# Attention and four experts on one core: where the weights' maxima come from, when preparations and chunk scales are issued, and a head's scores in one run

## The chip, the cores and the metric

The kernel runs on one core of one Trainium2 chip. The metric is the device time of one execution in microseconds (us); lower is better. The engines are named as in the profile: PE is TensorE (PEld is its weight load), DVE is VectorE, ACT is ScalarE, POOL is GpSimd, SP is SyncE, which here issues the DMAs.

## The reference

```python
def _attn_ref(q, k, v, f):                  # B, H, S, D = 4, 8, 576, 64
    scores = scale * np.matmul(q, k.transpose(0, 1, 3, 2))
    cum = np.cumsum(np.log(np.clip(f, 0.0001, 1.0)), axis=-1)
    decay = cum[:, :, :, None] - cum[:, :, None, :]
    scores = np.where(causal, -1000000000.0, scores + decay)
    attn = np.exp(scores - np.max(scores, axis=-1, keepdims=True))
    attn = attn / (np.sum(attn, axis=-1, keepdims=True) + 1e-09)
    return np.matmul(attn, v)

def _moe_ref(x, domain_probs, w1, w2):      # N, D, E, F = 2304, 512, 4, 1024
    p = domain_probs / (domain_probs.sum(-1, keepdims=True) + 1e-09)
    for e in range(E):
        h = np.maximum(x @ w1[e], 0.0)
        out += p[:, e:e + 1] * (h @ w2[e])
```

The attention output, heads side by side, is the x of the second function. The experts are dense: every row goes through all four.

## The kernel before

**Precision.** Each fp32 product is made of three passes: every operand is split into a high part and a low remainder, and high*high, high*low and low*high are added in PSUM. In the first sweep the parts are in the 32-bit matmul format; later they are 16-bit halves, which need scales that are powers of two. A scale comes from a maximum over the tensor: one per expert's weights (w_peek loads parts of the weights a second time, w_scale works the maxima out), one per chunk of x (x_scale).

**Attention.** A job is a batch, a pair of heads and one half of the queries: the first 256 rows (half 0, score tiles t = 0, 1) or the last 320 (half 1, t = 2, 3, 4 with 384, 512 and 576 keys). For a head, `prep` (L563 to L578) makes the high and low parts of q and k: hi on ACT, q2 (`q`, one buffer for each of the two heads of a pair), kl and the low part on POOL. `qk_pe` (L618) makes a tile's scores, two matmuls for each piece of columns, in a PSUM bank of the pool ps_a, which has four and also serves transposes, attention products and chunk scales. `qk_min` (L632) takes scores plus mask to SBUF and finds the minimum on DVE, `qk_exp` (L647) the exponential on ACT, `turn16` (L716, L717) scaled 16-bit copies, and SP issues DMA transposes of them (L726). `av_pair` (L818) multiplies with v two heads later.

**Experts.** x is cut into nine chunks of 256 rows. A step is a chunk, a pair of hidden units' blocks and its two matmul layers: `l1` (L1013), `gate` (relu and split on ACT and DVE, L1026 and L1027) and `l2` (L1046); DVE adds the scaled result to the chunk's accumulator (L1073). The first sweep (28 steps) runs chunks 0 to 2 in the 32-bit format with the attention of half 0; the second (52 steps) runs chunks 1 to 4 in halves with the attention of half 1. Then chunks 5 to 8 go through a stage of their own (L1284), which the change does not touch. `w_split` (L953 to L981) prepares a weight unit from its raw load `wr`, three buffers; units 0 to 31 are the first sweep's.

**Order.** The attention's pieces stand in a list (asteps), each with a cost; `pace` emits as many of them between two expert matmul groups as the costs and the chunks' due places allow. A tile framework then schedules each engine's instructions, and `tc.issue_after(i)` keeps what is issued inside behind instruction i on i's engine. `behind` and `paced` use it with a step's gate; `lows` are POOL's last preparations. When a chunk is complete, its `turn` enters the list:

```python
            (50, lambda: (top(), across())),
            (50, exponent),
            (150, finish),
```

Here top is the chunk's maximum on DVE (L261), across its transpose on PE into a row (L200, tile topx), exponent the power of two on DVE and a matmul that spreads it (L221). The steps at which expert e's weights are read for their maxima start at `PEEK = (1, 15, 31, 45)`, 16 steps each; 17 steps after each start w_scale reduces, stores and reads back the maxima (dw, tops).

## Time and profile before

| what | value |
|---|---|
| median of 3 runs | 925.6 us (924.88 to 925.85) |
| profiled execution, its own time | 930.58 us |
| span of its trace, first to last instruction | 928.8 us |
| mean granted clock of TensorE | 0.991 |
| instructions | 16629 |
| DMA | 159.45 MB, 172 GB/s in the mean |

The profiled execution is one run with the profiler on; its trace is what the rows below come from. A busy share is a mean over stages with different limits, so the windows and waits say more than the table of engines. An instruction's duration on PE includes its way through the array, so matmuls overlap: what one costs is read from start to start. In brackets behind an instruction stands the idle time of its engine before it, and what ended it.

### The profile page before, as it was taken

Reading aid. Unit: us, or ns where it says so; the run is one execution under the profiler, and the core shown is the slowest. Engines: PE = TensorE matmul, PEld = TensorE weight load, DVE = VectorE, ACT = ScalarE, POOL = GpSimd, SP = SyncE. Lnnn points to the kernel's source line nnn. Section 1 sums busy time; section 2 is a strip of 40 time slices with the busy share of each in tenths; the row PEclk is TensorE's granted clock in tenths of the full one; section 3 lists DMA queues with packets and bytes.
Section 4 is the critical chain, followed back from the end, with each engine's and each line's share of the span. In section 5 each row is a group of like instructions: output and inputs, shape, how many; then the busy total and the mean of one; then the engine's idle time right before and its main releaser. Section 6 shows DMA issues by size and latency. Waiting matters only on the chain.

```text
span 928.8 us, 16629 instructions
## 1 busy us (share of the span) xinstructions
PE 882.4 (95%) x5783; PEld 620.7 (67%) x5783; DVE 710.0 (76%) x1458; ACT 569.3 (61%) x1137; POOL 528.0 (57%) x528
## 2 busy tenths in 40 slices
PE   4899989998998899999999999899998999999998
PEld 3699879898876567666666666554455654666547
DVE  5768766686998888799888887676678647786487
ACT  5868766557676567767767775555665345653350
POOL 4655675655555552455635673785778527885060
PEclk9999989999999999999999999999999999999999
DMA  7457755455979969889999996744323324232003
GB/s 266 144 165 260 260 176 151 159 166 166 262 186 220 283 166 246 219 168 255 265 261 214 262 229 167 246 172 148 115 69 103 125 68 136 68 116 67 23 1 92
DMA packets 147508, 159.45 MB, mean 172 GB/s; under 512 B 86148, under 2 KB 107328, under 8 KB 147424
## 3 DMA queue, kind: packets, MB, share of 16 engines
q1 hardware_dynamic: 147424, 158.39, 61.1%
q8 instruction: 45, 0.74, 0.3%
q14 instruction: 39, 0.32, 0.1%
HBM read 117.30 MB, written 21.65 MB: 150 GB/s over the span
## 4 chain that ended last, share of the span: by engine, by line
PE 55%; POOL 12%; DVE 10%; ACT 7%; DMA 7%; issue 4%; SPq 0%; ACTq 0%; POOLq 0%; DVEq 0%
PE l L1046 16%; PE l L1013 15%; PE y L1284 8%; PE m L1284 7%; PE s L618 4%; POOL s L1344 4%; POOL wt L1178 3%; PE o L818 2%; POOL wu L1178 1%; DMA wr<-in_w 1%; DMA pk<-in_w 1%; DVE acc L1073 1%; DVE z L717 1%; DMA vr<-in_v 1%; ACT wt L1205 1%
## 5 line engine op out<-in xcount | busy, mean ns | idle before, releaser
L1013 PE MATMUL l<-y,w 128*128 128x256 f16 x1248 | 154.8, 275 | 2.7 <-ACT w L980 1.9
L647 ACT ACTIVATE p<-p,nm 128x576 f32<-128x576 f32 (+3 forms) x160 | 95.7, 599 | 82.7 <-DVE nm L632 77.9
L1013 PEld LDWEIGHTS <-w 128*128 128x128 f16 x1248 | 118.4, 99 | 34.2 <-issue 7.1
L1046 PE MATMUL l<-w,gh 128*128 128x512 f16 x408 | 122.2, 382 | 2.7 <-DVE acc L1073 2.0
L564 POOL CAST q<-raw 64x320 fp32r<-64x320 f32 (+1 forms) x56 | 28.1, 502 | 149.6 <-PE s L618 148.2
L1073 DVE SCALAR_TENSOR_TENSOR acc<-y,scg,acc 128x256 f32<-128x256 f32 (+1 forms) x164 | 81.1, 515 | 14.9 <-PE y L1284 14.7
L717 DVE SCALAR_TENSOR_TENSOR z<-p,rs,z 128x384 f16<-128x384 f32 (+3 forms) x128 | 82.4, 665 | 12.7 <-ACT z L716 11.3
L1284 PE MATMUL m<-rh,bs 128*128 128x512 f16 x256 | 86.6, 379 | 0.0
L572 POOL TENSOR_TENSOR kl<-raw,hi 64x576 fp32r<-64x576 f32 (+1 forms) x56 | 66.5, 1188 | 33.8 <-ACT hi L563 28.3
L618 PE MATMUL s<-hi 128*128 128x384 f32 (+1 forms) x192 | 74.9, 394 | 11.3 <-DVE hi L578 8.9
L632 DVE CUSTOM_DVE_ANT_0 p<-s,mask 128x288 f32<-128x288 f32 (+2 forms) x160 | 74.4, 473 | 13.3 <-PE s L618 12.7
L1210 POOL TENSOR_TENSOR bs<-wt,bs 128x512 f16<-128x512 f32 x32 | 38.1, 1192 | 71.3 <-ACT bs L1209 71.1
L1046 PE MATMUL l<-w,gl 128*128 128x512 f16 x204 | 77.3, 382 | 0.0
L716 ACT ACTIVATE z<-p,rs 128x384 f16<-128x384 f32 (+3 forms) x128 | 69.4, 589 | 7.0 <-DVE rs L678 3.4
L1027 DVE SCALAR_TENSOR_TENSOR gl<-l,gh 128x512 f16<-128x512 f32 (+1 forms) x80 | 54.8, 685 | 16.5 <-ACT gh L1026 15.8
L1013 PE MATMUL l<-xh,wh 128*128 128x256 f32 x224 | 65.1, 293 | 0.9 <-ACT xh L859 0.9
L957 POOL TENSOR_TENSOR wl<-wr,wh 128x512 fp32r<-128x512 f32 x48 | 61.7, 1313 | 7.3 <-ACT wh L953 3.6
L1284 PE MATMUL m<-rh,bw 128*128 128x512 f16 x191 | 64.4, 379 | 1.4 <-ACT r L1330 1.4
L1013 PE MATMUL l<-xl,wh 128*128 128x256 f32 x224 | 65.3, 292 | 0.0
L618 PE MATMUL s<-kl,q 66*128 66x384 f32 (+1 forms) x192 | 63.2, 334 | 2.2 <-DMA kl<-nc 2.2
L1013 PE MATMUL l<-xh,wl 128*128 128x256 f32 x224 | 65.2, 292 | 0.1
L1284 PEld LDWEIGHTS <-bs 128*128 128x128 f16 x384 | 37.6, 98 | 38.4
(385 smaller groups left out, 2344.0 us busy)
## 6 DMA issues: line engine op xcount, KB each, us to landing
wr<-in_w SPq DMA_DIRECT2D x90, 512.0 KB
pk<-in_w SPq DMA_DIRECT2D x64, 256.0 KB
wd<-w SPq DMA_DIRECT2D x32, 512.0 KB
raw<-in_qk SPq DMA_DIRECT2D x32, 448.0 KB
bw<-wd SPq DMA_DIRECT2D x32, 256.0 KB
bv<-wd SPq DMA_DIRECT2D x32, 256.0 KB
raw<-in_qk SPq DMA_DIRECT2D x24, 256.0 KB
vp<-in_v SPq DMA_DIRECT2D x10, 512.0 KB
```

Source lines behind the costliest of these rows:

```text
L572: eng.tensor_tensor(out=kl[:64, :wk], in0=r[:64, ko : ko + wk], in1=hi[:64, ko : ko + wk].bitcast(F32), op=ALU.subtract,)
L618: nc.tensor.matmul(out=ps[:, at : at + z - a], lhsT=lhsT, rhs=rhs, start=(m == 0), stop=(m == 1),)
L632: nc.vector.tensor_tensor_reduce(out=pt[:, a:z], in0=ps, in1=mask[:, m0 + a : m0 + z], scale=-0.125, scalar=BIG if n == 0 else nm[:, col : ...
L647: nc.scalar.activation(out=pt[:, :w_], in_=pt[:, :w_], func=AF.Exp, scale=-1.0, bias=self.nmax[hh][:, c : c + 1], accum_out=self.ssum[:, h ...
L716: nc.scalar.activation(out=o[:, 0], in_=x, func=AF.Copy, scale=sc)
L717: nc.vector.scalar_tensor_tensor(out=o[:, 1], in0=x, scalar=sc, in1=o[:, 0], op0=ALU.mult, op1=ALU.subtract)
L957: eng.tensor_tensor(out=wl[n][:, a:z], in0=r[:, a:z], in1=wh[n][:, a:z].bitcast(F32), op=ALU.subtract,)
L1013: nc.tensor.matmul(out=self.l1p[:, fi, :], lhsT=lhsT, rhs=rhs[:, k, :], start=(k == 0 and m == 0), stop=(k == 3 and m == 2),)
L1027: self.last = nc.vector.scalar_tensor_tensor(out=self.gl, in0=self.l1p, scalar=0.0, in1=self.gh.bitcast(F32) if wide else self.gh, op0=ALU ...
L1046: matmul(out=l2[tt], lhsT=lhsT, rhs=rhs, start=(self.ps == 0 and fi == 0 and m == 0), stop=(self.ps == 1 and fi == 1 and m == 2),)
L1073: nc.vector.scalar_tensor_tensor(out=acc[c][:, tt, d0:d1], in0=ps, scalar=sc, in1=acc[c][:, tt, d0:d1], op0=ALU.mult, op1=ALU.add,)
L1284: line.append(nc.tensor.matmul(**args))
```

## The change

Four things are edited. The weights of experts 2 and 3 are no longer loaded a second time for their maxima: w_split reduces the raw unit while it is in SBUF for the first sweep, and w_scale follows at steps 37 and 42. `prep` and `prep_v` are put behind the gate of the step before and behind POOL's last preparation. The chunk scale's chain has costs between its parts, and its PE instructions go behind the last l1 matmul so far. For half 1 a head's scores of all three tiles are issued in one run (`qk_head`), with the fourth bank saved: tile 4 is cut at key 448, and its last 128 columns share tile 2's bank.

```diff
--- before.py
+++ after.py
@@ -28,7 +28,8 @@
     ((1, 2, 3, 4), (1, 2, 3, 4), (2, 3, 4), (3, 4)),
 )
 WIDE = (0, 1, 2)
-PEEK = (1, 15, 31, 45)
+PEEK = (1, 15)
+SCALE = (18, 32, 37, 42)
 V_PEEK = 1
 PT = ("ptx", "pth", "ptl")
 TURN = ((1, 14), (2, 18), (3, 24), (4, 28))
@@ -482,12 +483,17 @@
                 out=yl[c], in0=xl[c].bitcast(F32), scalar=sc, in1=yl[c], op0=ALU.mult, op1=ALU.add
             )
 
+    def spaced(f):
+        with tc.issue_after(experts[-1].ins):
+            f()
+
     def turn(c):
 
         top, across, exponent, finish = x_scale(c, (c,))
         return [
-            (50, lambda: (top(), across())),
-            (50, exponent),
+            (0, top),
+            (900, lambda: spaced(across)),
+            (600, lambda: spaced(exponent)),
             (150, finish),
         ]
 
@@ -597,33 +603,38 @@
                 self.ssum = st_p.tile([128, 2, n], F32, tag="ssum", name=f"ss{self.nm}")
                 self.rs = st_p.tile([128, 2, n], F32, tag="rs", name=f"rs{self.nm}")
 
+        def qk_bank(self, hh, t):
+            return ps_a.tile([128, 512], F32, tag="a", name=f"s{self.nm}_{hh}_{t}")
+
+        def qk_piece(self, hh, t, a, z, ps):
+
+            o, i = self.qo + TOK0[t] - self.q0, TOK0[t] - self.q0
+            for m, (lhsT, rhs) in enumerate(
+                (
+                    (self.hi[hh][:, o : o + 128], self.hi[hh][:, self.ko + a : self.ko + z]),
+                    (q2[hh][:, i : i + 128], self.kl[hh][:66, a:z]),
+                )
+            ):
+                nc.tensor.matmul(out=ps, lhsT=lhsT, rhs=rhs, start=(m == 0), stop=(m == 1))
+            self.sp.setdefault((hh, t), []).append((a, z, ps))
+
         def qk_pe(self, hh, its):
 
             at = 512
             for t in its:
-                o = self.qo + TOK0[t] - self.q0
                 w_ = TOK0[t] + 128
-                cuts = ((0, w_),) if w_ <= 512 else ((0, w_ // 2), (w_ // 2, w_))
-                for n, (a, z) in enumerate(cuts):
-                    if at + z - a > 512:
-                        ps = ps_a.tile([128, 512], F32, tag="a", name=f"s{self.nm}_{hh}_{t}_{n}")
-                        at = 0
-                    i = TOK0[t] - self.q0
-                    for m, (lhsT, rhs) in enumerate(
-                        (
-                            (self.hi[hh][:, o : o + 128], self.hi[hh][:, self.ko + a : self.ko + z]),
-                            (q2[hh][:, i : i + 128], self.kl[hh][:66, a:z]),
-                        )
-                    ):
-                        nc.tensor.matmul(
-                            out=ps[:, at : at + z - a],
-                            lhsT=lhsT,
-                            rhs=rhs,
-                            start=(m == 0),
-                            stop=(m == 1),
-                        )
-                    self.sp.setdefault((hh, t), []).append((a, z, ps[:, at : at + z - a]))
-                    at += z - a
+                if at + w_ > 512:
+                    ps, at = self.qk_bank(hh, t), 0
+                self.qk_piece(hh, t, 0, w_, ps[:, at : at + w_])
+                at += w_
+
+        def qk_head(self, hh):
+
+            two, three, four = (self.qk_bank(hh, t) for t in (2, 3, 4))
+            self.qk_piece(hh, 2, 0, 384, two[:, :384])
+            self.qk_piece(hh, 4, 448, 576, two[:, 384:])
+            self.qk_piece(hh, 3, 0, 512, three)
+            self.qk_piece(hh, 4, 0, 448, four[:, :448])
 
         def qk_min(self, hh, t):
             pt, nm, col = self.p[hh, t], self.nmax[hh], 2 * (t - self.its[0])
@@ -889,10 +900,10 @@
 
         st = []
         if FIRST < n < len(heads) and heads[n][1] == 0:
-            st.append((0, heads[n][0].prep_v))
+            st.append((0, lambda j=heads[n][0]: held(j.prep_v)))
         if n + 1 < len(heads):
             j, hh = heads[n + 1]
-            st.append((0, lambda j=j, hh=hh: j.prep(hh)))
+            st.append((0, lambda j=j, hh=hh: held(lambda: j.prep(hh))))
         if n + 2 < len(heads):
             j, hh = heads[n + 2]
             st.append((0, lambda j=j, hh=hh: j.far(hh)))
@@ -900,8 +911,13 @@
         qs, ts, us = [], [], []
         if n < len(heads):
             j, hh = heads[n]
+            if j.half:
+                qs.append((1400, lambda j=j, hh=hh: j.qk_head(hh)))
             for t in j.its:
-                qs.append((TOK0[t] + 328, lambda j=j, hh=hh, t=t: j.qk_tile(hh, t)))
+                if j.half:
+                    qs.append((224, lambda j=j, hh=hh, t=t: (j.qk_min(hh, t), j.qk_exp(hh, t))))
+                else:
+                    qs.append((TOK0[t] + 328, lambda j=j, hh=hh, t=t: j.qk_tile(hh, t)))
             if j.half:
                 qs.append((0, lambda j=j, hh=hh: j.recip16(hh)))
                 for t in j.its:
@@ -910,7 +926,7 @@
                 qs.append((0, j.recip))
         if n - 2 >= FIRST and heads[n - 2][1] == 1 and heads[n - 2][0].half:
             j = heads[n - 2][0]
-            qs[2:2] = [(1000, j.av_pair), (0, j.out16)] + ready(n - 2)
+            qs[3:3] = [(1000, j.av_pair), (0, j.out16)] + ready(n - 2)
         if n - 2 >= FIRST and heads[n - 2][0].half == 0:
             j, hh = heads[n - 2]
             late_ = [(200, lambda j=j, hh=hh: j.av(hh))]
@@ -951,6 +967,14 @@
             wh[n] = w_p.tile([128, 1024], F32R, tag="wh", name=f"wh{n}")
             wl[n] = w_p.tile([128, 1024], F32R, tag="wl", name=f"wl{n}")
             nc.scalar.activation(out=wh[n], in_=r, func=AF.Copy)
+            if n // 8 >= len(PEEK):
+                nc.vector.tensor_reduce(
+                    out=wmax[:, :, n % 8, n // 8],
+                    in_=r.rearrange("p (k c) -> p k c", k=2),
+                    op=ALU.max,
+                    axis=AX.X,
+                    apply_absolute_value=True,
+                )
             eng = nc.vector if n in W_DVE else nc.gpsimd
             for a in (0, 512):
                 z = a + 512
@@ -993,6 +1017,7 @@
 
     acc = {}
     l2 = {}
+    experts = []
 
     class Step:
         def __init__(self, s, g, c, ps):
@@ -1010,13 +1035,14 @@
                 a = wh[n][:, k * 128 : (k + 1) * 128]
                 z = wl[n][:, k * 128 : (k + 1) * 128]
                 for m, (lhsT, rhs) in enumerate(((a, th), (a, tl), (z, th))):
-                    nc.tensor.matmul(
+                    i = nc.tensor.matmul(
                         out=self.l1p[:, fi, :],
                         lhsT=lhsT,
                         rhs=rhs[:, k, :],
                         start=(k == 0 and m == 0),
                         stop=(k == 3 and m == 2),
                     )
+            experts.append(i)
 
         def gate(self):
             wide = self.s == 0
@@ -1618,6 +1644,12 @@
     for n in range(len(W_SLOT), 6):
         w_split(n)
 
+    def held(f):
+        if prev is None:
+            f()
+        else:
+            paced(prev, f)
+
     def paced(t, f):
         with tc.issue_after(t.first.ins), tc.issue_after(t.last.ins), tc.issue_after(lows[-1].ins):
             f()
@@ -1631,10 +1663,10 @@
         for e, first_ in enumerate(PEEK):
             if 0 <= n - first_ < 16:
                 w_peek(e, n - first_)
-            if n == first_ + 17:
-                a_, b_ = w_scale(e)
-                behind(a_)
-                at_step(n + 3, b_)
+        if n in SCALE:
+            a_, b_ = w_scale(SCALE.index(n))
+            behind(a_)
+            at_step(n + 3, b_)
         if 0 <= n - V_PEEK < NV:
             v_peek(n - V_PEEK)
         if n == V_PEEK + NV + 1:
```

Where the instructions then stand is shown at three places; line numbers differ between the two programs by 1 to 32.

On PE, at the third chunk scale (topx), near the end of the first sweep; s are scores with batch left out (pair, half, head, tile), l expert products (sweep, pair of blocks, chunk, part), b the transpose of the softmax factors with which the chunk is completed. Before:

```order
L1013 MATMUL l_0_7_0_1_3083<-xh_471,wl_2969 128x256
L685 MATMUL b_3_0_3074<-ident,rb_3_0_2853 128x128 x2
L200 MATMUL topx_175<-ident,xmax 1x128
L618 MATMUL s_0_1_1_3_0_3125<-hi_0_1_1_2864 128x512
L618 MATMUL s_0_1_1_3_0_3125<-kl_0_1_1_2777,q_1_117 128x512
L618 MATMUL s_0_1_1_4_0_3153<-hi_0_1_1_2864 128x288
L618 MATMUL s_0_1_1_4_0_3153<-kl_0_1_1_2777,q_1_117 128x288
L618 MATMUL s_0_1_1_4_1_3156<-hi_0_1_1_2864 128x288
L618 MATMUL s_0_1_1_4_1_3156<-kl_0_1_1_2777,q_1_117 128x288
```

After:

```order
L1038 MATMUL l_0_7_2_0_3360<-xh_1635,wl_2591 128x256
L201 MATMUL topx_175<-ident,xmax 1x128
L618 MATMUL s_1_1_0_2_3280<-hi_1_1_0_3031 128x384
L618 MATMUL s_1_1_0_2_3280<-kl_1_1_0_2872,q_0_116 128x384
L618 MATMUL s_1_1_0_2_3280<-hi_1_1_0_3031 128x128
L618 MATMUL s_1_1_0_2_3280<-kl_1_1_0_2872,q_0_116 128x128
L618 MATMUL s_1_1_0_3_3281<-hi_1_1_0_3031 128x512
L618 MATMUL s_1_1_0_3_3281<-kl_1_1_0_2872,q_0_116 128x512
L618 MATMUL s_1_1_0_4_3282<-hi_1_1_0_3031 128x448
L618 MATMUL s_1_1_0_4_3282<-kl_1_1_0_2872,q_0_116 128x448
L1038 MATMUL l_0_7_2_0_3360<-xh_1635,wh_2598 128x256
```

Behind the transpose stood scores of an earlier head's tiles 3 and 4; now it stands among expert matmuls, 60 of them after b, and the eight score matmuls of one head follow each other.

On DVE, in the second sweep at the gate (gl) of blocks 2, chunk 3; p and nm are the minima's outputs, wmax the maxima of raw weights, acc the accumulation, z the 16-bit copies. Before:

```order
L632 ISA p_0_1_0_4_5288,nm_0_1_0_5289<-s_0_1_0_4_1_5406,mask,nm_0_1_0_5289 128x288
L632 ISA nm_0_1_0_5289 128x1
L632 ISA p_0_1_1_2_5426,nm_0_1_1_5429<-s_0_1_1_2_0_5458,mask 128x384
L632 ISA nm_0_1_1_5429 128x1
L1027 SCALAR_TENSOR_TENSOR gl_2_3_0_5452<-l_1_2_3_0_5390,gh_2_3_0_5451 128x512
L285 TENSOR_REDUCE wmax<-pk_2_5308 128x1
L1073 SCALAR_TENSOR_TENSOR acc_3053<-l_1_2_2_0_0_5344,scg,acc_3053 128x512
L675 TENSOR_SCALAR ss_0_1_5290<-ss_0_1_5290 128x3
L1073 SCALAR_TENSOR_TENSOR acc_3053<-l_1_2_2_0_1_5351,scg,acc_3053 128x512
```

After:

```order
L643 ISA p_0_1_0_4_5264,nm_0_1_0_5265<-s_0_1_0_2_5325,mask 128x128
L643 ISA nm_0_1_0_5265 128x1
L643 ISA p_0_1_0_4_5264,nm_0_1_0_5265<-s_0_1_0_4_5327,mask,nm_0_1_0_5265 128x448
L643 ISA nm_0_1_0_5265 128x1
L686 TENSOR_SCALAR ss_0_1_5266<-ss_0_1_5266 128x3
L689 RECIPROCAL rs_0_1_5267<-ss_0_1_5266 128x3
L1053 SCALAR_TENSOR_TENSOR gl_2_3_0_5413<-l_1_2_3_0_5353,gh_2_3_0_5412 128x512
L728 SCALAR_TENSOR_TENSOR z_3011<-p_0_1_0_2_5262,rs_0_1_5267,z_3011 128x3x128
L1099 SCALAR_TENSOR_TENSOR acc_3068<-l_1_2_2_0_0_5311,scg,acc_3068 128x512
L728 SCALAR_TENSOR_TENSOR z_3011<-p_0_1_0_3_5263,rs_0_1_5267,z_3011 128x4x128
L728 SCALAR_TENSOR_TENSOR z_3013<-p_0_1_0_4_5264,rs_0_1_5267,z_3013 64x4x128
L1099 SCALAR_TENSOR_TENSOR acc_3068<-l_1_2_2_0_1_5318,scg,acc_3068 128x512
```

The reduction of a second weight load (pk) between gate and accumulation is gone; the next head's minimum no longer stands ahead of the gate, and copies of this head stand between the two accumulations.

On SP, at the DMA transposes of the first batch's pair 2, second head (pt_2_1_1); wr, wd and vr are weights, stored weights and v, dw the store of an expert's maxima. Before:

```order
L538 DMA kl_0_1_0_3793<-ncd 2x576
L282 DMA pk_0_3832<-in_w 128x512
L513 DMA raw_0_1_1_3913<-in_qk 128x896
L538 DMA kl_0_1_1_3911<-ncd 2x576
L282 DMA pk_1_3927<-in_w 128x512
L726 DMA_TRANSPOSE pt_2_1_1_3767<-z_3015 128x6x128
L317 DMA dw_3922<-wm_3921 128x2
L726 DMA_TRANSPOSE pt_2_1_1_3767<-z_3015 128x8x128
L726 DMA_TRANSPOSE pt_2_1_1_3767<-z_3017 128x9x64
```

After:

```order
L954 DMA wr_3826<-in_w 128x1024
L544 DMA kl_0_1_1_3911<-ncd 2x576
L1013 DMA wd_138<-w_3820 128x2048
L523 DMA vr_0_1_3794<-in_v 128x640
L954 DMA wr_3834<-in_w 128x1024
L737 DMA_TRANSPOSE pt_2_1_1_3764<-z_3012 128x6x128
L737 DMA_TRANSPOSE pt_2_1_1_3764<-z_3012 128x8x128
L737 DMA_TRANSPOSE pt_2_1_1_3764<-z_3014 128x9x64
L1013 DMA wd_139<-w_3828 128x2048
L318 DMA dw_3929<-wm_3928 128x2
```

The two pk loads are gone, the three transposes follow each other, and the store of the maxima stands behind them instead of between.

## Rows read from the trace of the kernel before

**Rows 1.** The page, part 1: engine, busy us, share of span, instructions.

```profile
PE 882.4 (95%) x5783; PEld 620.7 (67%) x5783; DVE 710.0 (76%) x1458; ACT 569.3 (61%) x1137; POOL 528.0 (57%) x528
```

**Rows 2.** Windows of 25 us: busy us per engine, granted clock, DMA share, GB/s.

```profile
125.00:150.00 25.00, 24.15 (x141) 21.41 (x141) 19.44 (x47) 17.74 (x41) 14.46 (x17) 0.86 0.49 124
...
225.00:250.00 25.00, 22.27 (x130) 19.32 (x129) 21.45 (x53) 18.72 (x37) 16.42 (x16) 0.93 0.82 254
...
300.00:325.00 25.00, 22.08 (x156) 14.96 (x154) 21.97 (x48) 15.42 (x33) 12.83 (x13) 0.96 1.08 277
...
325.00:350.00 25.00, 25.00 (x178) 16.36 (x177) 21.51 (x50) 16.83 (x35) 12.51 (x12) 0.97 0.68 164
...
425.00:450.00 25.00, 25.00 (x186) 17.12 (x183) 22.95 (x54) 18.20 (x38) 14.87 (x15) 1.00 0.96 251
```

**Rows 3.** Waits, whole span: total us, times, longest us.

```profile
POOL q L564 <- PE s L618: 154.5, 36, 11.0
...
PE o L818 <- DMA pt<-z: 5.0, 2, 2.7
...
PE t L744 <- DVE pt L761: 3.2, 1, 3.2
...
PE topx L200 <- DVE xmax L261: 2.7, 1, 2.7
```

**Rows 4.** Timeline from 224 us, the third chunk-scale maximum: start, duration, engine, instruction.

```profile
229.40 1.21 DVE L261 TENSOR_REDUCE xmax<-xf 128x1 f32<-128x1024 f32 x1
...
230.66 0.27 PE L200 MATMUL topx<-ident,xmax 128*1 128x128 f32 x1 [2.73 <-DVE xmax L261]
```

**Rows 5.** Timeline at four places of the second sweep, from 286, 311 and 394 us.

```profile
296.75 1.69 PE L818 MATMUL o<-pt,v 128*64 128x320 f16 x27 [2.75 <-DMA pt<-z]
...
322.14 2.12 PE L818 MATMUL o<-pt,v 128*64 128x320 f16 x26 [2.23 <-DMA pt<-z]
...
395.08 1.34 DVE L285 TENSOR_REDUCE wmax<-pk 128x1 f32<-128x512 f32 x2 [2.89 <-DMA pk<-in_w]
...
412.24 0.59 PE L1046 MATMUL l<-w,gh 128*128 128x512 f16 x2 [1.65 <-DVE acc L1073]
```

**Rows 6.** Timeline of TensorE alone at two places with score matmuls.

```profile
300.76 0.38 PE L1046 MATMUL l<-w,gl 128*128 128x512 f16 x1
...
301.52 0.61 PE L1046 MATMUL l<-w,gh 128*128 128x512 f16 x2
...
119.46 0.28 PE L1013 MATMUL l<-xh,wh 128*128 128x256 f32 x1
119.57 0.22 PE L618 MATMUL s<-hi 128*128 128x128 f32 x1
119.63 0.28 PE L618 MATMUL s<-kl,q 66*128 66x128 f32 x1
119.75 0.33 PE L1013 MATMUL l<-xl,wh 128*128 128x256 f32 x1
```

**Rows 7.** VectorE groups by form: line, shapes, count, busy us, mean ns, idle before.

```profile
L285 DVE TENSOR_REDUCE wmax<-pk 128x1 f32<-128x512 f32 x64 | 42.9, 675 | 2.9 <-DMA pk<-in_w 2.9
...
L261 DVE TENSOR_REDUCE xmax<-xf 128x1 f32<-128x1024 f32 x6 | 7.2, 1209 | 1.9 <-ACT xf L872 1.9
```

**Rows 8.** Timeline around the stop of the first sweep, from 117 us.

```profile
123.14 1.06 ACT L953 ACTIVATE wh<-wr 128x1024 fp32r<-128x1024 f32 x1 [4.62 <-DMA wr<-in_w]
...
125.60 0.48 PE L744 MATMUL t<-ident,p 128*128 128x128 f32 x1 [3.20 <-DVE pt L761]
```

**Rows 9.** Timeline from 308 us: a head's last score matmul and its last minimum.

```profile
309.29 0.30 PE L618 MATMUL s<-kl,q 66*128 66x288 f32 x1
...
318.73 0.51 DVE L632 CUSTOM_DVE_ANT_0 p<-s,mask,nm 128x288 f32<-128x288 f32 x1
```

**Rows 10.** Line 818, attention products: count, ns min/median/max, first and last start.

```profile
L818 PE MATMUL o<-pt,v x448: 192/299/474, 249.4 to 582.6; 128*64 128x320 f16 x96, 128*64 128x192 f16 x30, 128*64 128x64 f16 x24
```

## Prediction

> **What bounds the kernel.** I read the page's table of engines first: TensorE is busy 95% of the span and VectorE 76% [rows 1]. The windows then show a flat middle: from 425 to 450 us TensorE has no idle time and runs 186 matmuls, 134 ns each, at a granted clock of 1.00 [rows 2]. There a change can gain only by streaming fewer or better packed columns. Time can be won where TensorE stops. The list of waits names what it stops for, outside the start-up and the last stage: the attention product for its transposed probabilities (5.0 us), one chunk-scale transpose for its maximum (2.7 us), a transpose in the first sweep for VectorE (3.2 us) [rows 3]. Each stop is followed by lost clock. The windows holding or following these stops show 0.86 (125 to 150), 0.93 (225 to 250), 0.96 and 0.97 (300 to 350) [rows 2]; the share missing from 1.00 times 25 us is 3.5, 1.75, 1.0 and 0.75 us. Of the two levels (1.2 and 2.4 GHz), a part of the window was at the lower.
>
> **The change, part by part.** All is summed against the profiled execution's 930.58 us (span 928.8), 4.98 above the median of 925.6, and the same 4.98 is then taken off.
>
> **Chunk scale.** In before, the transpose of chunk 3's maximum stands directly behind the matmuls that made the chunk. VectorE starts the maximum at 229.40, takes 1.21 us, and TensorE stands 2.73 us until 230.66, with six score matmuls behind it in its queue [rows 4]. The order now puts 60 expert matmuls between, 8 us at 134 ns. The maximum's work is unchanged, so it is hidden under those matmuls: -2.73, and with it the 1.75 us of clock: -4.5 in all. If the cover fails, this is 0. The other chunks' transposes show no such stop; the last one, for chunks 5 to 8, is not spread and I leave it. These steps now cost 1650 instead of 250 in the planner, so the attention of a chunk runs somewhat ahead of the expert steps; no instruction is added.
>
> **Scores in one run, and the attention products.** A head's eight score matmuls, issued in three places before, now go together. The product of a pair follows two heads later and needs the DMA transposes of both heads, which need scores, minimum, exponential and scaled copies. The two waits are 2.75 and 2.23 us [rows 5]. In the new order the last scores of these two heads (pairs 2 and 3 of the first batch) stand 31 and 51 expert matmuls earlier, their products 6 and 15 earlier. That is 25 and 36 matmuls of extra distance, at 134 ns 3.4 and 4.8 us, more than either wait. A third stop of 1.65 us, at 412, is the expert product waiting for VectorE's accumulation [rows 5]; it goes under the next part. With the clock of 300 to 350 (1.75) the three are worth 8.4 us. The distance helps only as far as VectorE and the transposes keep up, so I take three quarters, -6.3; the ends are 0 and -8.4.
>
> **Streaming price of the run.** Columns are the same (1472 per operand pair), but the fourth tile is cut 448 and 128 instead of 288 and 288. Four matmuls of 288 columns: the one before starts at 300.76 and streams 512 columns, 0.213 us at 2.4 GHz, so the four hold TensorE from 300.97 to 301.52: 0.55 us against 0.48 of columns, 0.07 lost [rows 6]. Two matmuls of 128: from 119.46 plus 0.107 to 119.75, 0.183 us against 0.107, 0.076 lost [rows 6]. Before, a head loses this 0.07 and, by the same 0.018 a matmul, 0.07 more at its two other places of two matmuls: 0.14. After: 0.018 for each of eight matmuls and 0.02 more for each short one, 0.18. The difference, 0.04 times 32 heads, is +1.3 us; the ends are 0 (the saved switches pay for it) and +2.4 (32 times 0.076).
>
> A rule of the Trainium skill speaks against the short pieces: its page "TensorE: Matmul & The Clock Gate", section "Back-to-back issue gap", gives a sustained spacing of about 81 ns at 128 columns, where streaming alone would be near 53. By it the 64 short matmuls would cost 1.8 us; the row above gives 38 ns each, 2.4 us as the end just named, so the two nearly agree and the row is used.
>
> **Raw maxima.** Removed: 32 loads of 256 KB and 32 reductions of 675 ns, 21.6 us of VectorE. Added: 16 reductions of 128x1024, 1209 ns by the nearest row, 19.3 us [rows 7], in the first sweep, where VectorE has room: 19.4 and 21.5 of 25 us in the first two windows shown [rows 2]. They wait for no load of their own: ScalarE waits for the same ones. The removed ones stood in the second sweep, where VectorE has 21.5 to 23 of 25 us busy [rows 2]. There VectorE stood 2.89 us for such a load at 395 and took two reductions [rows 5], and one stands in the order right before the accumulation that TensorE then waits for. Freed of them it is not late at 412. This gain is in the three quarters above; later, TensorE is full and the removal is worth nothing. Bounds on the added ones: 0 (hidden), +4.8 if each of four weight loads is held by one reduction, 1.2 each. I take 0. The scales of experts 2 and 3 are made 11 and 20 steps earlier with the same instructions and DMAs; their use comes later, so nothing waits: 0.
>
> **Preparations behind gates.** GpSimd stands 154.5 us for q2 to be released by scores [rows 3], with weight preparation queued behind. Issuing the scores together frees q2 about a head earlier, and the gate order makes preparations yield to the gates' copies on ScalarE and VectorE. TensorE itself waits for none of this in the second sweep: 0. In the first sweep the 3.2 us stop at 122 comes from ScalarE standing 4.62 us for a weight load [rows 8], held up by GpSimd's late subtraction. The new order has the same preparation ahead of the same subtraction there, and the same load ahead of the same exponential. I take 0; if it went, it would be worth 3.2 and 3.5 of clock, 6.7; if such a stop is added, the same the other way.
>
> **Banks.** A run takes three of four PSUM banks at once, where four were taken one after another. I charge +1.0 between 0 and the slower rival's price.
>
> **Sum:** -4.5 - 6.3 + 1.3 + 1.0 = -8.5. 930.6 - 8.5 = 922.1 profiled, 917.1 as a median.
>
> **The rivals.**
> *Only the chunk wait goes* (the transposes keep their waits, because VectorE's queue and not the scores sets them): -4.5 + 1.3 + 1.0 = -2.2, 923.4. For it: one of those stretches has VectorE 22 us of 25 busy [rows 2]. Against: the scores' order.
> *The first sweep's stop goes too*: -8.5 - 6.7, 910.4. For it: the loads it waits for come from the queue that the preparations shared. Against: the order there.
> *Bank waits, slower.* The last scores of a head at 309.29 have their minimum started only at 318.73 [rows 9], 9.4 us and 0.5 for itself; pairs come every (581 - 249) / 15 = 22.1 us [rows 10], so a head every 11. The next run needs two banks of the last, so the room is about 1.1 us. Once VectorE is more than that late, TensorE stands with all experts' matmuls behind. The new order also sets two runs of the first batch only 24 expert matmuls apart, about 4 us. Three stops of 3 us and one loss of clock as at 125 (3.5) are +12.5 over the forecast: 929.6. The deciding point is two such stops. The Trainium skill's page "PSUM — Partial Sum Buffer", section "PSUM bank collisions raise a hardware error", asks that banks and not addresses be guarded, by which the packed bank stays taken until both its tiles are read; no row of before shows a packed bank of the second sweep.
> *The change does not do what it says*: the maximum is as late as the transpose and the products' wait is replaced: 925.6.
>
> **How the numbers follow.** Chances: forecast 0.45, only the chunk wait 0.16, first stop too 0.14, bank waits 0.16, no effect 0.09. The predicted time is the forecast's, 917.1. The range leaves out the tails: 908 (the first stop partly gone, all three product stops gone) to 929 (just short of three bank stops). A change within 0.2% (1.9 us) can't be told from none. Faster: 0.45 + 0.14 + 0.10 of the 923.4 case, which sits near that bound: 0.69. Same: the other 0.06 of it and 0.08 of no effect: 0.14. Slower: bank waits and the last 0.01: 0.17.
>
> **What would show it.** Right: no wait of the chunk transpose in the list; the attention product's wait under 1.5 us; no dip of the clock in 225 to 350; VectorE about 2 us less busy in all. Wrong: score matmuls waiting for minima (banks), weight copies waiting longer for loads in the first sweep (the added readers), or product waits unchanged while scores come earlier. The stop at 122 should still be there.

## The result, and the profile after

The changed kernel takes 931.34 us (median of 4 runs, 931.08 to 931.49) against 925.24 us before: the ratio is 1.0066, with an interval from 1.0048 to 1.0083. It is 6.1 us slower, where 8.5 us faster was forecast. The profiled execution takes 931.08 us, its span is 929.3 us.

The page's table of engines, part 1, hardly differs from [rows 1]; VectorE is not 2 us less busy but 0.9 more (two traces of the kernel before differ by 0.7):

```profile
PE 881.4 (95%) x5783; PEld 621.0 (67%) x5783; DVE 710.9 (77%) x1442; ACT 568.7 (61%) x1137; POOL 524.6 (56%) x528
```

The list of waits after (total us, times, longest) answers to [rows 3]:

```profile
PE l L1072 <- DVE acc L1099: 5.9, 6, 3.4
PE l L1072 <- ACT gh L1052: 3.5, 3, 2.2
...
PE t L755 <- ACT p L658: 2.8, 4, 1.5
...
PE o L829 <- DMA pt<-z: 1.2, 3, 0.6
```

The wait of the chunk transpose (topx) is gone, that of the attention products fell from 5.0 to 1.2 us, and the 3.2 us stop of the first sweep is not there. New are expert products (l) that wait for VectorE's accumulation and for ScalarE's gate. The windows, with columns as in [rows 2]:

```profile
125.00:150.00 25.00, 24.79 (x166) 22.27 (x164) 20.58 (x49) 17.31 (x43) 11.23 (x17) 1.00 0.47 150
225.00:250.00 25.00, 22.02 (x132) 18.98 (x132) 22.82 (x54) 14.50 (x31) 15.59 (x15) 1.00 0.83 254
300.00:325.00 25.00, 23.01 (x170) 15.61 (x169) 19.98 (x49) 18.11 (x39) 9.51 (x11) 1.00 1.07 232
325.00:350.00 25.00, 24.56 (x179) 16.75 (x178) 20.84 (x52) 14.52 (x29) 16.06 (x17) 1.00 0.68 148
575.00:600.00 25.00, 21.12 (x127) 12.90 (x126) 16.89 (x30) 13.48 (x24) 17.24 (x16) 0.93 0.66 218
600.00:625.00 25.00, 21.58 (x118) 11.72 (x117) 13.30 (x16) 10.93 (x18) 20.84 (x21) 0.93 0.56 192
```

The dips of the clock between 225 and 350 us are gone, as forecast, but from 225 to 250 TensorE still lacks 3 us of work. And where the second sweep passes into the last stage, for which the prediction has no term, there are two windows at 0.93, where the kernel before has one:

```profile
575.00:600.00 25.00, 22.32 (x163) 15.10 (x162) 14.06 (x26) 10.81 (x20) 15.37 (x16) 0.93 0.69 190
600.00:625.00 25.00, 24.46 (x139) 13.31 (x138) 18.80 (x23) 14.27 (x25) 20.94 (x19) 1.00 0.54 204
```

The timeline after, VectorE's and TensorE's rows:

```profile
607.74 1.71 DVE L1191 SCALAR_TENSOR_TENSOR rl<-rx,xsc,rh 128x512 f16<-128x512 f32 x1 [0.24 <-ACT rh L1190]
...
609.69 1.71 DVE L1191 SCALAR_TENSOR_TENSOR rl<-rx,xsc,rh 128x512 f16<-128x512 f32 x1 [0.24 <-ACT rh L1190]
...
611.33 0.68 DVE L1053 SCALAR_TENSOR_TENSOR gl<-l,gh 128x512 f16<-128x512 f32 x1
...
611.93 0.73 DVE L1099 SCALAR_TENSOR_TENSOR acc<-l,scg,acc 128x512 f32<-128x512 f32 x1
...
612.72 1.01 PE L1072 MATMUL l<-w,gh 128*128 128x512 f16 x2 [3.42 <-DVE acc L1099]
```

VectorE makes the low parts of the last stage's x (rl) ahead of a gate (gl) and an accumulation (acc) of the second sweep; TensorE stands 3.42 us for that accumulation.

**Where the time lies.** Every variant has the same 2868 expert matmuls in the two sweeps, in nearly the same order: against the kernel before, 60 to 377 places of a variant's trace hold a matmul of another kind, but up to the 1001st the kinds are counted alike to within six, and up to the 2701st exactly. So equal counts mark nearly equal work. The table gives, for each traced execution, the time up to the 1001st of them (start), from there to the 2701st (sweep), from there to the 61st of the last stage's line (pass), and on to its 1801st (last). Medians and ratios are those of all runs; each experiment's ratio goes against runs of the kernel before on its chip.

```
kernel                    median  ratio [interval]          start  sweep  pass   last
before (rows 1 to 10)     925.24                            257.5  325.7  43.7  297.4
after                     931.34  1.0066 [1.0048, 1.0083]   256.4  321.9  49.1  297.5
e1 before again           925.15  1.0008 [0.9990, 1.0027]   251.7  322.0  43.8  297.5
e2 no run                 923.09  0.9978 [0.9961, 0.9995]   258.1  317.6  44.4  297.5
e3 only run               934.05  1.0097 [1.0071, 1.0123]   255.3  328.6  49.1  297.5
e4 no raw                 928.48  1.0040 [1.0023, 1.0058]   253.9  322.5  49.2  297.5
e5 AHEAD 3                931.67  1.0070 [1.0046, 1.0095]   256.0  322.0  48.2  297.5
e6 gates, spread          920.83  0.9958 [0.9943, 0.9972]   250.8  322.6  43.8  297.5
e7 only raw               930.35  1.0053 [1.0033, 1.0072]   263.8  318.8  44.5  297.5
e8 only spread            919.65  0.9938 [0.9914, 0.9961]   249.8  323.0  44.0  297.5
e9 more reductions        934.02  1.0105 [1.0079, 1.0132]   262.8  323.6  43.8  297.5
e10 no second loads       919.87  0.9942 [0.9920, 0.9963]   255.2  316.7  44.4  297.5
e11 run, transition       923.79  1.0001 [0.9982, 1.0020]   256.0  322.2  43.1  297.5
e12 run, spread costs     926.26  1.0020 [0.9999, 1.0040]   257.3  324.1  43.2  297.4
e13 whole, transition     926.76  1.0025 [1.0001, 1.0049]   259.8  321.6  43.4  297.4
e14 before, AHEAD 3       929.71  1.0051 [1.0028, 1.0073]   250.8  323.0  52.4  297.4
e15 raw and spread        924.21  0.9987 [0.9966, 1.0008]   260.8  318.6  43.9  297.4
e16 spread and run        923.60  0.9994 [0.9971, 1.0017]   247.8  328.8  43.1  297.4
e17 raw later             929.25  1.0058 [1.0035, 1.0082]   259.1  320.7  43.9  297.4
e18 raw later, spread     926.69  1.0025 [1.0010, 1.0041]   261.1  317.2  44.3  297.4
```

Start and sweep are single executions of a kernel whose runs spread over 6 to 12 us (before: 920.1 to 932.0 in the widest set), so they are read over several traces; in the two traces of the kernel before, pass and last repeat within about 0.1 us.

### The profile page after: what moved, and what is told of

The parts are those of the page before. It is cut to its first block, busy times and chain, and to the rows that moved or that the text cites. A ratio compares the mean times of both kernels' runs of the same rounds, so it can differ in the third digit from the quotient of the medians.

```text
span 929.3 us, 16535 instructions
## 1 busy us (share of the span) xinstructions
PE 881.4 (95%) x5783; PEld 621.0 (67%) x5783; DVE 710.9 (77%) x1442; ACT 568.7 (61%) x1137; POOL 524.6 (56%) x528
## 4 chain that ended last, share of the span: by engine, by line
PE 39%; POOL 12%; DVE 5%; ACT 5%; issue 4%; DMA 1%; SPq 0%; POOLq 0%; DVEq 0%; ACTq 0%
PE l L1072 10%; PE l L1038 10%; PE y L1310 6%; PE m L1310 6%; POOL s L1370 4%; POOL wt L1204 3%; PE s L618 3%; PE o L829 2%; POOL wu L1204 2%; POOL bs L1236 1%; DVE acc L1099 1%; ACT r L1356 1%; ACT wt L1231 1%; DVE h L1345 1%; DVE rl L1191 1%
## 5 line engine op out<-in xcount | busy, mean ns | idle before, releaser
L1038 PE MATMUL l<-y,w 128*128 128x256 f16 x1248 | 151.2, 274 | 3.3 <-ACT w L1004 2.5
L658 ACT ACTIVATE p<-p,nm 128x576 f32<-128x576 f32 (+2 forms) x160 | 95.5, 597 | 74.2 <-DVE nm L643 73.4
L618 PE MATMUL s<-hi 128*128 128x384 f32 (+1 forms) x192 | 69.3, 369 | 12.2 <-DVE hi L584 8.8
L643 DVE CUSTOM_DVE_ANT_0 p<-s,mask 128x128 f32<-128x128 f32 (+1 forms) x160 | 66.6, 442 | 14.1 <-PE s L618 13.3
L1072 PEld LDWEIGHTS <-gh 128*128 128x128 f16 x408 | 38.5, 98 | 42.9 <-issue 7.8
## 6 DMA issues: line engine op xcount, KB each, us to landing
pk<-in_w SPq DMA_DIRECT2D x32, 256.0 KB
bw<-wd SPq DMA_DIRECT2D x32, 256.0 KB
bv<-wd SPq DMA_DIRECT2D x32, 256.0 KB
raw<-in_qk SPq DMA_DIRECT2D x24, 256.0 KB
```

The source lines that it names most:

```text
L618: nc.tensor.matmul(out=ps, lhsT=lhsT, rhs=rhs, start=(m == 0), stop=(m == 1))
L643: nc.vector.tensor_tensor_reduce(out=pt[:, a:z], in0=ps, in1=mask[:, m0 + a : m0 + z], scale=-0.125, scalar=BIG if n == 0 else nm[:, col : ...
L658: nc.scalar.activation(out=pt[:, :w_], in_=pt[:, :w_], func=AF.Exp, scale=-1.0, bias=self.nmax[hh][:, c : c + 1], accum_out=self.ssum[:, h ...
L1038: i = nc.tensor.matmul(out=self.l1p[:, fi, :], lhsT=lhsT, rhs=rhs[:, k, :], start=(k == 0 and m == 0), stop=(k == 3 and m == 2),)
L1072: matmul(out=l2[tt], lhsT=lhsT, rhs=rhs, start=(self.ps == 0 and fi == 0 and m == 0), stop=(self.ps == 1 and fi == 1 and m == 2),)
```

## The experiments

**The kernel before again (e1).** No edit.

> The kernel before, nothing changed, for a second trace. The prediction was summed against a profiled execution of 930.58 us while the median of the other runs is 925.6. Theory 'unusual trace': the 3.2 us stop at 122 us with its low clock (0.86 in 125 to 150), 6.7 us in all, belongs to that one execution; a new trace has a span near 924, no such stop, and its end of the attention some 5 us earlier. Rival 'profiler': a profiled execution of this kernel is always some 5 us longer; then the span is again 928 to 929 with the same stops. The ratio is 1.000 within 0.001.

Its trace spans 919.5 us, shorter than the 924 expected. The windows:

```profile
125.00:150.00 25.00, 25.00 (x172) 22.85 (x171) 18.52 (x47) 18.07 (x43) 16.99 (x19) 1.00 0.60 174
225.00:250.00 25.00, 25.00 (x143) 21.74 (x143) 23.10 (x56) 17.77 (x35) 13.12 (x12) 0.93 0.99 265
300.00:325.00 25.00, 22.86 (x170) 15.71 (x169) 22.62 (x51) 14.43 (x29) 10.61 (x12) 1.00 1.08 278
325.00:350.00 25.00, 25.00 (x180) 16.43 (x179) 23.12 (x52) 19.57 (x40) 13.26 (x13) 1.00 0.79 182
```

No 0.86 after 125 us, no dip in 300 to 350: these did not recur and belonged to the execution that the prediction was summed on. The rival falls. From 300 to 325 TensorE lacks 2.1 us of work at a clock of 1.00, so a stop need not cost clock. Usual are the chunk transpose's 2.7 us, and product waits of 3.0 us in all for 5.0.

**Scores by tile again (e2), and the run alone (e3).** The edit on the kernel after, or on the kernel before the other way round:

```diff
-            if j.half:
-                qs.append((1400, lambda j=j, hh=hh: j.qk_head(hh)))
...
+                qs.append((TOK0[t] + 328, lambda j=j, hh=hh, t=t: j.qk_tile(hh, t)))
...
-            qs[3:3] = [(1000, j.av_pair), (0, j.out16)] + ready(n - 2)
+            qs[2:2] = [(1000, j.av_pair), (0, j.out16)] + ready(n - 2)
```

> The changed kernel with scores by tile as before; raw maxima, gates and the spread chain stay. Theory 'transition': the run of scores lets the attention of the last heads end some 30 expert matmuls earlier, so that VectorE works on the last stage's x (rl) ahead of the last gates and accumulations, which makes the 3.6 us stop at 609 us and its clock; without the run VectorE's order there is that of before, the stop is gone and the time is 921 to 925. Rival 'first sweep': the raw maxima and gates make many small stops between 75 and 275 us, and they stay: 929 to 932.

> The kernel before with only the scores of a head in one run (and products placed accordingly). Theory 'transition': the stop of 3 to 4 us near 609 us and low clock behind it appear, the product waits shrink from 5.0 us: 926 to 931. Rival 'first sweep': this edit alone costs nothing or gains what was forecast for it (5 us net): 919 to 925.

Without the run 923.09, with it alone 934.05: the run costs 8.2 us within the change and 9.0 alone. In e3 the wait is the one seen after:

```profile
PE l L1071 <- DVE acc L1098: 6.7, 6, 3.4
```

The pass takes 49.1 to 49.2 us in the three traces with the run so far (after, e3, e4) and 43.7 to 44.4 in those without: 5 us. The rest, some 3, is to be looked for in the sweep (321.9 after, 317.6 in e2).

**Without raw maxima (e4).** On the kernel after:

```diff
-PEEK = (1, 15)
-SCALE = (18, 32, 37, 42)
+PEEK = (1, 15, 31, 45)
+SCALE = (18, 32, 48, 62)
```

> The changed kernel with the weights of experts 2 and 3 loaded a second time again for their maxima, as before; run of scores, gates and spread chain stay. Theory 'transition': the stop near 609 stays; 930 to 933, as the reductions in the second sweep come back beside a full TensorE. Rival 'first sweep': the small stops between 75 and 275 us go away, 4 to 6 us less: 925 to 927.

928.48, 2.9 less than after, between the two: the stop at the pass stays (3.4 us), the stops of the first sweep get fewer. Both theories hold a part.

**One step later (e5).** AHEAD is the planner's lead: with 3 for 4 the attention may end one expert step later.

```diff
-AHEAD = 4
+AHEAD = 3
```

> The changed kernel whole, with one constant other (AHEAD 3 for 4: the planner lets the attention end one expert step later). In the order of the instructions this puts VectorE's work at the transition to the last stage back to that of before. Theory 'transition and gates' (the run of scores costs 8 us: 5.0 at the transition, where all three traces with it lose 4.8 to 5.0 us between the same two matmuls, and 3 in the second sweep, where expert products wait for gates and accumulations): the 3.6 us stop is gone and the time is 926 to 927. Rival 'all in the sweep' (the stop at the transition only takes up slack that is lost anyway): 929 to 932.

931.67, no gain: the first theory missed. VectorE's order was put back, but in ScalarE's the scaling of the next weights (wt), which waits for GpSimd, now came ahead of the copy r:

```profile
615.87 1.33 ACT L1231 ACTIVATE wt<-wt,wsc 128x512 f32<-128x512 f32 x2 [3.59 <-POOL wt L1204]
617.11 0.57 ACT L1356 ACTIVATE r<-m 128x512 f32<-128x512 f32 x1
...
617.74 0.38 PE L1310 MATMUL m<-rh,bs 128*128 128x512 f16 x1 [3.18 <-ACT r L1356]
```

The stop had only moved to another queue; the pass still takes 48.2.

**Gates and spread chain (e6), raw maxima alone (e7), spread chain alone (e8).** Each is the kernel before with those hunks of the change's diff: `held` for the gates, PEEK, SCALE and the reduction in w_split for the raw maxima, `turn` and `spaced` for the chain.

```diff
-            (50, lambda: (top(), across())),
-            (50, exponent),
+            (0, top),
+            (900, lambda: spaced(across)),
+            (600, lambda: spaced(exponent)),
```

> The kernel before with preparations behind gates and the spread chunk scale chain only. From the medians so far (raw maxima cost 2.9 within the change, the run of scores 8.2) these two should gain about 5: 920. Rival: the gain of the three edits without the run (2.0) is all they have, and the raw maxima cost nothing where the run is absent: 923.

> The kernel before with only the raw units' maxima. Theory 'first sweep readers': the 16 reductions hold weight buffers and gates in the first sweep, several stops of 0.5 to 1 us more between 75 and 200 us, and the second sweep gives back less: 927 to 929. Rival 'hidden', as the prediction had it: 924 to 926, with the 1.7 us stop before the accumulation at about 400 us gone.

> The kernel before with only the chunk scale chain spread. The prediction gave this 4.5 us: 920 to 921. Rival 'replaced wait': in the traces with the spread chain the first layer-two product behind b now waits 2.4 to 2.9 us for ScalarE's gate at the place where the transpose waited 2.7 for the maximum, so nothing is gained there: 924 to 926.

The spread chain gains 5.3 us, a little more than forecast; with the gates 4.1, so these cost about 1 by the medians, which the intervals don't tell from 0. The raw maxima cost 5.4, beyond the upper end of +4.8. In e7, VectorE's group of the new reductions, and two of the waits:

```profile
L960 DVE TENSOR_REDUCE wmax<-wr 128x2 f32<-128x1024 f32 x16 | 19.0, 1212 | 5.8 <-DMA wr<-in_w 5.8
```

```profile
DVE wmax L960 <- DMA wr<-in_w: 5.8, 4, 2.8
...
PE topx L201 <- DVE xmax L262: 3.8, 1, 3.8
```

The time of a reduction is as costed (1.212 us), but VectorE also stands 5.8 us for the loads, and the chunk's transpose waits 1.1 us longer for its maximum than in [rows 3].

**The two halves of the raw maxima (e9, e10).** In e9 the reductions are added and the second loads stay; in e10 the second loads go and nothing replaces them:

```diff
+            if n // 8 >= 2:
+                nc.vector.tensor_reduce(
+                    out=wmax[:, :, n % 8, n // 8],
...
-PEEK = (1, 15, 31, 45)
+PEEK = (1, 15)
+SCALE = (18, 32, 48, 62)
...
-            nc.vector.tensor_reduce(out=m, in_=wmax[:, :, :, e], op=ALU.max, axis=AX.X)
+            nc.vector.tensor_reduce(out=m, in_=wmax[:, :, :, e % 2], op=ALU.max, axis=AX.X)
```

> The kernel before, with the 16 reductions of raw units added and the second loads kept as well (their maxima overwrite the same values later). This prices the added work alone. Theory 'first sweep readers': with the raw maxima alone 930.35, of which the second sweep gives back 2 to 4, the reductions cost 7 to 9 in the first sweep, so 932 to 934, and the third chunk transpose waits 4 us for its maximum instead of 2.7. Rival 'hidden', as the prediction had it: 924 to 926.

> The kernel before without the second loads and reductions for experts 2 and 3, and nothing in their place (the scales of experts 2 and 3 are made from the maxima of experts 0 and 1, so this leaves out their own maxima). This prices the removed work alone. Theory: the 1.7 us stop before the accumulation at 400 us goes and part of the product waits: 2 to 4 us less, 921 to 923. Rival: TensorE is full in the second sweep and nothing is gained: 925.

The reductions alone cost 9.4 us, the removal alone gains 4.8, more than expected; the difference, 4.6, is near the 5.4 of both. The cost lies in the start: the nine traces with the reductions take 256.0 to 263.8 us there, 259.8 in the mean, the eleven without 247.8 to 257.5, 253.3 in the mean. GpSimd's work beside them hardly slows (a low part wl takes 1313 ns before and 1335 in e9), so a slower neighbour is not the price. In e10 the windows that held the second product wait and the accumulation's stop of [rows 5] are full; one product wait stays (1.9 us, before 300):

```profile
300.00:325.00 25.00, 25.00 (x186) 17.01 (x184) 22.11 (x55) 17.00 (x35) 14.12 (x15) 1.00 0.96 240
...
400.00:425.00 25.00, 25.00 (x191) 16.87 (x190) 21.85 (x53) 18.61 (x38) 10.52 (x12) 1.00 0.72 200
```

**The run with its pass mended (e11), and its vector work spread (e12).** On e3: AHEAD 3, and the second weight pair's scaling behind the copy r. e12 also shares the costs out (445 for 224 at each tile).

```diff
+            if p == 1:
+                put_off.extend(split_1(p))
+                return
...
+                    if q == 0:
+                        for f_ in put_off:
+                            with tc.issue_after(mark[-1].ins):
+                                f_()
...
-                qs.append((1400, lambda j=j, hh=hh: j.qk_head(hh)))
+                qs.append((800, lambda j=j, hh=hh: j.qk_head(hh)))
```

> The kernel before with the run of scores (934.05 by itself), the planner's constant AHEAD 3 for 4, and the scaling of the last stage's second weight pair put behind ScalarE's first copy r, so that both VectorE and ScalarE keep the order of before at the transition. Theory 'transition and lumps': 4 to 5 us of the loss go, 929 to 930; what stays, 4, is in the second sweep. Rival 'all in the sweep': the stop moves once more and the time stays at 933 to 935.

> The kernel of the run before it, with the planner's costs of a head shared out differently: 800 for the scores and 445 for each tile's minimum and exponential, instead of 1400 and 224 (sum 2135 for 2072). The matmuls of the scores still go together; the minima and exponentials no longer come as one lump on VectorE and ScalarE. Theory 'transition and lumps': expert products no longer wait for gates and accumulations behind the lump, 924 to 926. Rival 'banks or streaming' (the run itself costs): 928 to 930, as without the sharing out.

e11 takes 923.79, 10.3 us less than e3 and more than expected; the pass is 43.1, 6.0 shorter, and what gave the other 4.3 is not shown. Against the kernel before, the run with its pass mended neither gains nor loses (ratio 1.0001). e12 is not better than e11: the lump of a head's vector work is not what the run costs in the sweep. That part of the theory falls.

**The whole change mended (e13), and AHEAD alone (e14).** e13 is the kernel after with e11's edit (AHEAD 3 and `put_off`), e14 the kernel before with `AHEAD = 3`.

> The whole change with the same two corrections at the transition as in the run of scores alone (AHEAD 3, and the second pair's scaling behind ScalarE's copy r). There they gave back 10.3 us, of which the traces show 6.0 at the transition. Theory 'sum of parts': the changed kernel's 931.3 less 5 to 6 at the transition, 925 to 926; the raw maxima (5.4 alone) and the spread chain (-5.3 alone) about cancel. Rival 'the run costs in the sweep as well': 928 to 930.

> The kernel before with AHEAD 3 for 4 alone, a control. In the order of its instructions ScalarE's scaling of the last stage's weights, which waits for GpSimd, comes ahead of its first copy r, as in the whole change with AHEAD 3, where TensorE then stood 3.3 us. Theory 'transition': the same stop near 608 to 614 us and the clock behind it, 3 to 5 us slower than before, 928 to 930, without any run of scores. Rival 'AHEAD 3 gains in the sweep' (and this is what helped the run of scores): 918 to 923.

e13 takes 926.76, 4.6 less than after; its pass fell by 5.7. e14, without any run of scores, takes 929.71, 5.0 more than before, and has e5's stop. Its pass of 52.4 also holds 27 attention products, which in the other traces come ahead of it, so it is not to be set beside theirs:

```profile
615.92 1.33 ACT L1205 ACTIVATE wt<-wt,wsc 128x512 f32<-128x512 f32 x2 [3.59 <-POOL wt L1178]
617.16 0.58 ACT L1330 ACTIVATE r<-m 128x512 f32<-128x512 f32 x1
...
617.79 0.38 PE L1284 MATMUL m<-rh,bs 128*128 128x512 f16 x1 [3.18 <-ACT r L1330]
```

So the order of the queues at the pass sets these 5 us, whatever brings it about, and AHEAD 3 gains nothing by itself.

**Parts together (e15, e16).** e15 joins raw maxima and spread chain, e16 the spread chain and the mended run.

> The kernel before with raw maxima and the spread chain, without the run of scores and the gates. Alone the one cost 5.4 and the other gained 5.3. Theory 'shared stop': part of the cost of the raw maxima is the third chunk transpose, which waits 4.0 instead of 2.9 us because a raw reduction stands ahead of the chunk's maximum, with a window at a clock of 0.86; spread, this is hidden, so the sum is less than the parts: 921 to 923. Rival 'additive': 925.

> The kernel before with the spread chain and the run of scores with its corrected transition, without raw maxima and gates. Alone they gave 919.65 and 923.8. Theory 'lump at the gate': with the run, ScalarE's scaled copies of a head (2.2 us) stand ahead of the gate at 226 to 229 us, the expert product there waits 2.4 to 3.2 us in all three kernels with the run, so the spread chain loses most of its gain: 921 to 924. Rival 'additive': 918 to 919, the fastest of all.

e15 takes 924.21: the parts add, and beside the raw maxima the spread chain gains 6.1 us (e7 has 930.35). Yet its trace has stops near the third chunk scale where e8 has none. The windows from 200 to 250 us of e8, then of e15:

```profile
200.00:225.00 25.00, 25.00 (x171) 23.05 (x170) 21.18 (x53) 15.54 (x32) 13.82 (x15) 1.00 0.61 174
225.00:250.00 25.00, 25.00 (x159) 22.24 (x158) 23.55 (x56) 18.75 (x37) 14.10 (x12) 1.00 0.72 196
```

```profile
200.00:225.00 25.00, 23.78 (x158) 20.91 (x157) 21.31 (x55) 14.73 (x34) 15.90 (x19) 1.00 0.54 166
225.00:250.00 25.00, 20.18 (x117) 17.15 (x116) 21.41 (x49) 16.91 (x34) 18.41 (x18) 0.86 0.77 216
```

Near the third chunk scale the four traces with the spread chain and no raw maxima (e4, e6, e8, e16) have no stop over 1 us. The six with both (after, e2, e5, e13, e15, e18) stand 2.2 to 3.0 us, the first expert product behind the factors' transpose waiting for ScalarE's gate, and e15 and e18 stand 1.9 and 1.3 us more for the chunk's maximum. In e15, and of e3's list of waits the one whose longest stands at that place (228 us):

```profile
231.40 0.50 PE L1062 MATMUL l<-wh,gh 128*128 128x512 f32 x1 [2.25 <-ACT gh L1042]
...
234.69 0.37 PE L201 MATMUL topx<-ident,xmax 128*1 128x128 f32 x1 [1.87 <-DVE xmax L262]
```

```profile
PE l L1071 <- ACT gh L1051: 4.4, 4, 3.0
```

e3 and e11 have the run, but neither raw maxima nor spread chain, and they stand there too, so raw maxima are not the only thing that makes that gate late. The mechanism named for e16 is thus wrong: its time came as expected (923.60), but it has no stop there, its start is the shortest of all, 247.8, and in its trace the loss lies in the sweep, 328.8. Beside the mended run the spread chain gains nothing clear (ratio 0.9994 in e16, 1.0001 in e11). Why is open.

**Reductions of wh, a step later (e17), and with the spread chain (e18).**

```diff
-                    in_=r.rearrange("p (k c) -> p k c", k=2),
...
+                at_step(
+                    step + 1,
+                    lambda: nc.vector.tensor_reduce(
...
+                        in_=wh[n].bitcast(F32).rearrange("p (k c) -> p k c", k=2),
```

> The kernel before with raw maxima alone, but each reduction reads the high part that ScalarE has made (wh), one expert step later, instead of the raw unit when it lands. The work on VectorE is the same 16 times 1.21 us; VectorE no longer stands for the load (5.8 us in four waits, longest 2.8, with the raw unit) and the raw buffer is not held for it. Theory 'VectorE stands for the load': most of the 9.4 us that the reductions cost in the first sweep goes, and the removed second loads gain 4.8: 921 to 924. Rival 'VectorE's time': the 19.4 us of reductions are themselves what makes gates and the chunk maximum late, and the time stays at 929 to 931.

> The same with the spread chunk scale chain as well (raw unit's maxima and spread chain together measured 924.2). Theory 'VectorE stands for the load': the gains of the two parts add, 917 to 919, the fastest so far. Rival 'VectorE's time': 923 to 925.

929.25 and 926.69: in e17 the rival's time came, and e18 lies above both ranges; the theory's gain is in neither. VectorE's group in e17:

```profile
L962 DVE TENSOR_REDUCE wmax<-wh 128x2 f32<-128x1024 f32 x16 | 19.4, 1213 | 1.2 <-ACT wh L958 1.2
```

It stands 1.2 us ahead of them for 5.8, and the time is 1.1 less, which the intervals of e7 and e17 don't tell from 0. So most of the cost stays when the standing goes, and goes with VectorE's 19 us of work. Which of the things behind it in the queue costs most stays open.

## Why the prediction was wrong

The step that failed first is a path without a term. The prediction follows TensorE's stops up to 412 us and costs the run of scores only where its matmuls and products stand; of the pass into the last stage it says only that the chain for chunks 5 to 8 "is not spread and I leave it". The run cost 5 us there. The second is the raw maxima, taken at 0: they cost 5.4 alone and 2.9 within the change. The pass alone doesn't explain the miss: mended, the whole change still takes 926.76 (e13), where 917.1 was forecast.

- **The pass.** In the run the last head's last scores stand behind 2580 expert matmuls instead of 2616, so the attention ends earlier, the last stage's x is ready earlier, and the scheduler puts VectorE's work on it ahead of the last gates: +5 us, shown by e3, e11 and e13. The three signs of being right on TensorE (no wait of the chunk transpose, product waits under 1.5 us, no dip of the clock from 225 to 350) came true, and this loss stood outside of where it looked. Of them the clock from 300 to 350 proves nothing, as it shows 1.00 in e1 too.
- **Chunk scale, -4.5.** Right alone (-5.3 in e8), and beside raw maxima (-6.1, e15 against e7). Within the change the wait of the transpose went, but the gate's product stands 2.2 us near that place, and beside the mended run the gain is gone (e16). No run takes the spread chain alone out of the change, so what the term was worth there, and why it shrinks beside the run, is not shown.
- **Raw maxima, 0.** The price of the added work was 9.4 (e9), twice the upper end. "VectorE has room: 19.4 and 21.5 of 25 us" read busy time as slack; "They wait for no load of their own" was wrong by 5.8 us of standing in e7, though in e17 most of the cost stays without it. The sign named for these readers, weight copies waiting longer for loads, did not come (4.9 us in all after, 7.9 before), and the cost came all the same. The removal was worth 4.8 (e10) by itself. It was placed inside the run's -6.3.
- **Products and VectorE freed, -6.3.** The product waits did fall, by 3.8 us against [rows 3] and 1.8 against e1. With the two charges on the run, +1.3 and +1.0, -4.0 was summed; the run alone with its pass mended gives nothing (e11). What shortens the sweep is the removal of the loads: without them, and without the run, it takes 316.7 to 320.7 us in six traces (e2, e7, e10, e15, e17, e18), with them 322.0 to 325.7 in six. The run adds to it: 321.6 to 322.0 in the three traces with run and without loads, 3.5 more in the mean.
- **Streaming, +1.3.** Under-sized. In the trace after, one head's run on TensorE:

```profile
288.29 0.42 PE L618 MATMUL s<-hi 128*128 128x384 f32 x1
288.55 0.34 PE L618 MATMUL s<-kl,q 66*128 66x384 f32 x1
288.73 0.23 PE L618 MATMUL s<-hi 128*128 128x128 f32 x1
288.79 0.27 PE L618 MATMUL s<-kl,q 66*128 66x128 f32 x1
288.90 0.45 PE L618 MATMUL s<-hi 128*128 128x512 f32 x1
289.19 0.40 PE L618 MATMUL s<-kl,q 66*128 66x512 f32 x1
289.42 0.37 PE L618 MATMUL s<-hi 128*128 128x448 f32 x1
```

The short pair holds TensorE 0.17 us (288.73 to 288.90) for 0.107 of columns, as costed, but the matmul behind it is late as well: 0.29 for 0.213, where the next one takes 0.23. The row behind those of [rows 6] showed the same before: the matmul of 256 columns at 119.75 takes 0.17 us to the next start, where such matmuls follow each other every 0.117 elsewhere in that trace, and the price was read only up to its start.

```profile
119.92 0.28 PE L794 MATMUL o<-pt,v 128*128 128x256 f32 x1
```

Over the heads of this form the loss is 0.246 us a head (median of 25 heads), against 0.151 before (0.063, 0.046 and 0.042 at the three places); 0.095 times 32 is +3.0, above the end of +2.4. That would be most of the run's 3.5 in the sweep, but it is a sum over start times: no run takes the scores together with the cuts of before.

- **Preparations and banks.** The gates cost about 1 by the medians, not told from the 0 taken. Score matmuls wait 0.4 us for a minimum, once in the trace after: the slower rival named the wrong wait.
- **The base.** The stop at 122 us and the dips of 300 to 350 belonged to that one execution; 4.98 us were taken off the sum, but the product term was sized on its waits. The clock was added to each wait, and that does not hold either: after, 3.0 us of work are missing from 225 to 250 at a clock of 1.00.

The prices of the parts alone do not add up to the change: run 9.0, raw maxima 5.4, chunk scale -5.3 and gates about 1 make +10, and +6.1 was measured.

The spread chain alone (e8, 919.65) is the fastest version timed that computes everything, 0.62% under the kernel before and 1.3% under the changed one.

## What to carry to other kernels

Where a scheduler orders the queues, a moved piece of work also moves what follows its end: compare each engine's order at the next stage's beginning, on all engines, and price a stop there. A busy share of 80% was no cover here for added work on an engine whose results others wait for; add the work alone and time it. Take a second trace of the kernel before, so that the terms are sized on stops that recur.

## Not expected of the hardware

From the 61st to the 1801st matmul of the last stage all twenty traces agree (297.4 to 297.5 us), while two executions of the same program differ by 6 us up to the 1001st expert matmul (257.5 and 251.7). And a 512-column fp32 matmul behind two of 128 columns took 0.29 us from start to start (288.90 to 289.19), against 0.23 behind one of its own length (289.19 to 289.42).
